# Attention and gated feed-forward in one kernel: two chunks' split weights kept across block borders, k and v laid out as four positions in 128 partitions plus a rest, three smaller stores

## The chip, the cores and the metric

One Trainium2 chip, one of its cores. The metric is device time in microseconds (us), the median of three runs of the program. The kernel before takes 946.88 us (945.2 to 952.26).

## What is computed

Inputs are q, k, v (8 batches x 8 heads x 576 positions x 64) and the weights of a gated feed-forward layer (512 to 1536 to 512), all f32.

```python
q_s = softmax(q, axis=-1)                  # over the 64 features
k_s = softmax(k, axis=2)                   # over the 576 positions
kv  = einsum('bhsd,bhse->bhde', k_s, v)
x   = einsum('bhsd,bhde->bhse', q_s, kv)   # -> 4608 tokens x 512
xn  = x / sqrt(mean(x*x) + 1e-06) * rms_g
out = (silu(xn @ w_gate) * (xn @ w_val)) @ w_out
```

A batch gives 576 tokens; the feed-forward layer (called the FFN here) works on nine blocks of 512 tokens.

## The kernel before, in words

**Precision.** Each f32 operand of a matmul is split in two halves, a high one (a cast to TensorE's fp32r type) and a low one (value minus high half), and each product is made of three matmuls: high by high, high by low, low by high. So the weights are split too, chunk by chunk.

**Order.** Nothing is scheduled by a compiler. A long string, ORDER, lists every step as `name.arguments`, with an engine behind a colon (S = SyncE, A = ScalarE, D = VectorE, P = GpSimd) where the step doesn't take its usual one. Each step issues its instructions when the string comes to it, so the string is the order of every engine and of each queue. Loads of q, k and v and most stores to memory go out on SyncE's queue (SP), one instruction after the other; one that has to wait holds up all behind it. In the program every DMA on SP also waits for the landing of the DMA eight places ahead of it on SP.

**FFN.** The first three blocks (0 to 2) are computed plainly: 36 steps s = 0 to 35, where block = s div 12 and the chunk of 128 of the 1536 hidden features is s mod 12. Step s has `f1.s` (gate and value products, L996), `g_mul`, `silu`, `h_mul`, `h_hi`, `h_lo` (the hidden values and their halves, L1008, L1005, L411, L1017) and `f2.s` (product with w_out, L1033). Before `f1.s`, the chunk's weights are split: `w_hi.s` (a cast of 128x1024, L411), `w_lo.s.0` and `w_lo.s.1` (two subtractions of 128x512, L920), and for `f2.s` `o_hi.s` (a cast of 128x512) and `o_lo.s` (a subtraction of 128x512, L928). The tiles `w` and `o` for them have two buffers each. In block 2 the chunks 6 to 11 (s = 30 to 35) don't split again: `w_back` and `o_back` read halves back that were kept in memory.

During block 1 (s = 12 to 23) the halves are also stored to memory: `w_keep.s` (L940, 1024 KB into `wd`, half of a slot for a pair of chunks) and `o_keep.s` (L944, 512 KB into `od`), together with sums of quarters of the weights (`s_add`, `s_hi`, `s_lo`, `s_keep`, L969 to L981) and copies of the raw weights (`r_keep`, L1254). The last six blocks run as three pairs with Strassen's scheme on these stored pieces, read back on GpSimd's queue. Of an odd chunk's two stored quarters, the first (A21) is read again only by `w_back`.

**Attention.** It runs in between, on batches 1 to 7 (batch 0 comes first, in another layout). For batch b and head pair g: `k_load` (three DMAs on SP, L505 and L509), `k_max` (DVE, L547), `k_tr` (a transposition on PE, L563), `k_top` (DVE maximum, tile `kx`, L568), `k_rows` (PE, L573), `k_sub` (DVE, L579), `k_exp` (ACT, L583), `k_mm` (PE, L600); `v_load` is four DMAs (L535, L536) and `v_ones` two memsets (L542, L543). The 576 positions of a head lie in 128 partitions as five positions each in 64 partitions and, in the other 64, four new positions and one taken twice, whose row in v's tile is zero. `q_load` is eight DMAs in runs of 128 bytes (L670), followed by `q_max` (DVE, L736), `q_exp` (ACT, L757), `q_mul` (POOL) and so on. `store` scales an output tile (ACT or DVE, L416) and stores it (SP, L1040).

Of the kernel before, what the change touches and what calls it, by code (L numbers as in the profile page):

```python
# [86 lines left out]
q_max2.2.2 n_rows.1 q_sub.2.2:P store.0.2:A k_top.2.1 g_mul.12 k_rows.2.1 s_lo.1.1:P k_mm.2.0 q_exp.2.2 k_sub.2.1
w_keep.13:S w_hi.14.0.2:A r_keep.1 f1.13.0 k_eps.2.0 q_half2.2.1 s_add.1.4:P k_load.2.2 k_exp.2.1 q_max.2.3 silu.12
k_rec.2.0 w_lo.14.0:P k_mm.2.1 v_ones.2.2 w_lo.14.1:D kv_hi.2.0:A q_half.2.3 s_add.2.1:P s_keep.1.1:S v_load.2.2
store.0.3:A h_mul.12 s_add.0.1:P g_mul.13 f1.13.1 h_hi.12:A q_sum.2.2 o_hi.13:A h_lo.12:P kv_lo.2.0 q_half2.2.2  # L90
s_add.0.3:P q_max2.2.3 q_sum2.2.2 q_sum2.2.1 k_eps.2.1 q_rec.2.2 k_rec.2.1 v_ones.2.3 o_lo.13:D q_sub.2.3:D k_load.2.3
s_lo.1.2:D q_rec.2.1 q_mul.2.1:P o_keep.13:S w_keep.14:S store.0.1:A s_hi.1.4:A silu.13 f2.12 kv_hi.2.1:A q_exp.2.3
f1.14.0 s_lo.1.4:D k_max.2.2 s_hi.2.1:A q_lo.2.0:P o_hi.15:A kv_lo.2.1 w_hi.15.0.2:A s_keep.1.2:S h_mul.13 k_tr.2.2
v_load.2.3 q_x.2.0 s_add.2.2:P k_top.2.2 q_sum.2.3 k_rows.2.2 x_sq.2.0 q_t.2.1 f1.14.1 o_lo.15:P x_hi.2.0:A k_sub.2.2
q_hi.2.1:A x_lo.2.0 q_mul.2.2:P k_exp.2.2 q_half2.2.3 h_hi.13:A q_lo.2.1:P g_mul.14 k_mm.2.2 silu.14 q_x.2.1
# [1382 lines left out]
```

## Time and profile before

| | us |
|---|---|
| median of 3 runs (lowest, highest) | 946.88 (945.2, 952.26) |
| profiled execution, its own time | 944.05 |
| its span, first to last instruction | 941.8 |
| PE (matmul) busy | 924.7 |
| DVE, ACT, POOL busy | 729.5, 467.4, 532.8 |
| mean granted TensorE clock | 0.997 |

The rows below come from the one profiled execution; times in them count from the start of its span. PE is TensorE, DVE VectorE, ACT ScalarE, POOL GpSimd. "SPq" is SP's queue of DMA issues. A row of the chain of work gives start, duration, and what ran.

### The profile page before, as it was taken

How to read it: one execution, taken by the hardware profiler on the slowest of the kernel's cores; microseconds unless marked ns; L12 is line 12 of the kernel's file. 1: busy time of each engine (PE TensorE's matmuls, PEld its weight loads, DVE VectorE, ACT ScalarE, POOL GpSimd, SP SyncE). 2: the span in 40 equal slices, each digit the busy share in tenths (PEclk: the TensorE clock that was granted, in tenths of full speed). 3: DMA queues.
4: the chain of work that ended last, by engine and by line, in shares of the span. 5: the costliest groups of instructions: out<-in, count | busy, mean ns of one | idle time of the engine just before them, and what ended most of it. 6: DMA issues, size and time to landing. Idle time of an engine off the chain costs nothing.

```text
span 941.8 us, 14336 instructions
## 1 busy us (share of the span) xinstructions
PE 924.7 (98%) x4621; PEld 748.9 (80%) x4621; DVE 729.5 (77%) x1526; ACT 467.4 (50%) x748; POOL 532.8 (57%) x546
## 2 busy tenths in 40 slices
PE   8999999999999998999999999999999999999998
PEld 6687877887877886888888888888888888888886
DVE  6989879988978996877877788775458975646586
ACT  4998848765678764655644364322215522111241
POOL 4887978877677995667764535433532423332403
PEclk9999999999999999999999999999999999999999
DMA  9997528989977999798995699888665778855255
GB/s 237 285 249 227 157 47 283 295 269 311 289 247 210 240 249 239 192 254 223 254 248 181 198 286 282 279 292 296 187 210 176 218 193 264 271 203 179 66 158 90
DMA packets 210298, 212.65 MB, mean 226 GB/s; under 512 B 132144, under 2 KB 171568, under 8 KB 205616
## 3 DMA queue, kind: packets, MB, share of 16 engines
q1 hardware_dynamic: 187568, 122.86, 47.7%
q0 software_dynamic: 16320, 88.09, 29.9%
q10 hardware_dynamic: 6336, 0.79, 0.6%
q8 instruction: 37, 0.61, 0.3%
q14 instruction: 37, 0.30, 0.1%
HBM read 161.35 MB, written 50.33 MB: 225 GB/s over the span
## 4 chain that ended last, share of the span: by engine, by line
PE 83%; DMA 7%; DVE 3%; ACT 2%; issue 2%; SPq 2%; POOL 0%; DVEq 0%; ACTq 0%
PE ps_gv L1145 18%; PE ps_gv L996 14%; PE ps_o L1145 12%; PE ps_o L1033 7%; PE ps_a L1145 7%; PE ps_o L1354 6%; PE ps_o L1238 4%; PE ps_a L1354 4%; PE ps_gv L1354 3%; DMA qt<-in_q_dram 2%; PE ps_a L1238 2%; PE ps_gv L1238 2%; DMA w<-in_v_dram 2%; PE ps_a L600 2%; PE ps_a L808 2%
## 5 line engine op out<-in xcount | busy, mean ns | idle before, releaser
L996 PE MATMUL ps_gv<-xh,w 128*128 128x512 f32 x576 | 191.8, 399 | 1.1 <-DVE gs L1008 1.1
L1145 PE MATMUL ps_gv<-x,ring 128*128 128x512 f32 x576 | 143.0, 392 | 0.0
L996 PEld LDWEIGHTS ps_gv<-xh,w 128*128 128x128 f32 x576 | 108.5, 188 | 26.9 <-DVE gs L1008 2.1
L1145 PEld LDWEIGHTS ps_gv<-x,ring 128*128 128x128 f32 x576 | 107.0, 188 | 23.0
L996 PE MATMUL ps_gv<-xl,w 128*128 128x512 f32 x288 | 112.6, 392 | 0.0
L1166 DVE TENSOR_TENSOR tmp<-tmp,ps_gv 128x512 f32<-128x512 f32 x84 | 57.3, 684 | 49.5 <-PE ps_gv L1145 47.8
L1145 PE MATMUL ps_o<-x,ring 128*128 128x512 f32 x360 | 85.1, 389 | 0.0
L1118 POOL DMA_DIRECT2D ring<-wd x54 | 31.0, 575 | 91.2 <-PE ps_o L1145 34.1
L1145 PEld LDWEIGHTS ps_o<-x,ring 128*128 128x128 f32 x360 | 67.6, 188 | 14.2
L1033 PE MATMUL ps_o<-o,hh 128*128 128x512 f32 x288 | 73.5, 396 | 0.0
L996 PEld LDWEIGHTS ps_gv<-xl,w 128*128 128x128 f32 x288 | 54.5, 189 | 10.7 <-issue 0.4
L1033 PEld LDWEIGHTS ps_o<-o,hh 128*128 128x128 f32 x288 | 52.9, 188 | 11.8 <-ACT ot L416 0.7
L1166 DVE TENSOR_TENSOR tmp<-tmp,ps_o 128x512 f32<-128x512 f32 x42 | 28.7, 685 | 29.1 <-PE ps_o L1145 25.7
L920 POOL TENSOR_TENSOR w<-w,w 128x512 fp32r<-128x512 f32 x34 | 45.9, 1359 | 8.2 <-ACT w L411 7.6
L411 ACT CAST hh<-gs 128x512 fp32r<-128x512 f32 x48 | 29.6, 617 | 30.4 <-DVE gs L1008 16.0
L1033 PE MATMUL ps_o<-o,hl 128*128 128x512 f32 x144 | 39.7, 399 | 4.3 <-DVE hl L1017 4.3
L1118 POOL DMA_DIRECT2D w<-wd x18 | 10.1, 559 | 58.0 <-PE ps_a L1145 37.8
L547 DVE TENSOR_REDUCE cm<-kt 128x128 f32<-128x640 f32 x28 | 36.7, 1312 | 3.1 <-DMA kt<-in_k_dram 3.0
L1145 PE MATMUL ps_a<-x,w 128*128 128x512 f32 x144 | 36.9, 392 | 0.0
L1017 POOL TENSOR_TENSOR hl<-gs,hh 128x512 fp32r<-128x512 f32 x21 | 28.1, 1339 | 15.2 <-DMA qt<-in_q_dram 6.0
L1145 PE MATMUL ps_a<-x,ring 128*128 128x512 f32 x144 | 36.7, 390 | 0.0
L1033 PEld LDWEIGHTS ps_o<-o,hl 128*128 128x128 f32 x144 | 27.4, 191 | 10.9 <-DVE hl L1017 4.7
(632 smaller groups left out, 2320.3 us busy)
## 6 DMA issues: line engine op xcount, KB each, us to landing
...
```

What stands on the lines that cost most here:

```text
L411: (e.copy if e is nc.scalar else e.tensor_copy)(dst, src)
L547: nc.vector.tensor_reduce(out=cm, in_=kt_[b, g].rearrange("p h j d -> p h d j"), axis=AX.X, op=ALU.max)
L600: nc.tensor.matmul(pk[h * D:(h + 1) * D, :D + 1], lhsT=ke[:, h, j], rhs=vt[:, j, h], start=(j == 0), stop=(j == CH - 1))
L920: on(nc.gpsimd).tensor_tensor(out=w[:, :, 1], in0=halves(s % NF, a, 1)[:, 0], in1=w[:, :, 0].bitcast(F32), op=ALU.subtract)
L996: nc.tensor.matmul(pd[s], lhsT=w[:, a, c // 2, m, c % 2 * P:c % 2 * P + P], rhs=X[j, c][x], start=(n == 1), stop=(n == 3 * NKT))
L1017: on(nc.gpsimd).tensor_tensor(out=hl, in0=g_[s], in1=h_[s][0].bitcast(F32), op=ALU.subtract)
L1033: nc.tensor.matmul(po[t], lhsT=a[:, t * P:(t + 1) * P], rhs=w, start=(i == 0 and n == 0), stop=(i == NF - 1 and n == len(terms) - 1))
L1118: nc.gpsimd.dma_start(t, src.rearrange("p a b f -> p (a b f)"))
L1145: nc.tensor.matmul(abc[p, i, m, b], lhsT=src[:, h, c * P:(c + 1) * P], rhs=operand(o, c, x), start=first and n == 0, stop=n == 5, skip_gro ...
L1166: nc.vector.tensor_tensor(out=dst, in0=ux[u + (src,)], in1=abc[u + (b,)], op=ALU.add)
L1238: nc.tensor.matmul(pa[p, t, k], lhsT=a[:, k * P:(k + 1) * P], rhs=w, start=(c == 0 and n == 0), stop=(c == NF - 1 and n == 2))
L1354: nc.tensor.matmul(qacc[p, b, x], lhsT=ws[l][x], rhs=h[m], start=first and i == 0 and n == 0, stop=i == NH - 1 and n == 2, skip_group_chec ...
```

## The change

1. A table CHUNK gives the chunk of each step. Block 1 runs chunks 10, 11, 2 to 9, 0, 1 instead of 0 to 11; blocks 0 and 2 are as before. So the last two chunks of a block are the first two of the next one, and `held(s)` makes steps 12 and 13 use the tiles of steps 10 and 11, and steps 24 and 25 those of 22 and 23. The 16 split steps (`w_hi`, two `w_lo`, `o_hi`, `o_lo`) of s = 12, 13, 24 and 25 are gone.
2. `k_load` is two DMAs instead of three: positions 0 to 511 as four per partition in all 128 partitions (both heads, runs of 1024 bytes), and the last 128 positions as a fifth one per partition (runs of 256 bytes; 64 of them are positions already loaded). Before, its runs were 1280 bytes. `v_load` is three DMAs instead of four, in the same layout: four positions in 128 partitions for each head, and the last 64 positions of both heads in the upper 64 partitions. The bytes are the same.
3. `w_keep` of an odd chunk that no `w_back` reads (chunks 1, 3 and 5) stores its second quarter alone: 512 KB instead of 1024 KB, three times.

The order of matmuls on PE is the same.

```diff
-silu.11 v_ones.2.0 v_load.2.0 q_load.2.3 w_hi.12.0.2:A o_hi.12:D o_hi.11:D n_sum.1 w_hi.13.0.2:A h_mul.11 w_lo.12.0:D
-o_lo.11:D kv_lo.1.2:P k_tr.2.0 w_lo.12.1:P f1.12.0 q_hi.2.0:A q_sub.2.1:P w_keep.12:S r_keep.5 kv_lo.1.3:P q_exp.2.1
+silu.11 v_ones.2.0 v_load.2.0 q_load.2.3 o_hi.11:D n_sum.1 h_mul.11 o_lo.11:D kv_lo.1.2:P k_tr.2.0 f1.12.0 q_hi.2.0:A
+q_sub.2.1:P w_keep.12:S r_keep.5 kv_lo.1.3:P q_exp.2.1 f1.12.1 r_keep.2 s_add.1.1:D r_keep.0 n_t.1 s_add.1.2:P
...
     def k_load(b, g):
...
-        head = k[b, hs].rearrange("h s d -> h (s d)")
-        low = head[:, :CH * LOW * D].rearrange("h (p e) -> p h e", p=LOW)
-        nc.sync.dma_start(kt[:LOW].rearrange("p h j d -> p h (j d)"), low)
-        for h in range(2):
-            first = k[b, 2 * g + h, CH * LOW - 1:CH * LOW]
-            over = bass.AP(tensor=first.tensor, offset=first.offset, ap=[[(CH - 1) * D, P - LOW], [1, CH * D]])
-            nc.sync.dma_start(kt[LOW:, h].rearrange("p j d -> p (j d)"), over)
+        nc.sync.dma_start(kt[:, :, :CH - 1].rearrange("p h j d -> p h (j d)"),
+                          k[b, hs, :REST].rearrange("h (p j) d -> p h (j d)", j=CH - 1))
+        nc.sync.dma_start(kt[:, :, CH - 1], k[b, hs, S - P:].rearrange("h p d -> p h d"))
...
-            nc.sync.dma_start(vt[:LOW, :, h, :D], src[:CH * LOW].rearrange("(p j) d -> p j d", j=CH))
-            nc.sync.dma_start(vt[LOW:, 1:, h, :D], src[CH * LOW:].rearrange("(p j) d -> p j d", j=CH - 1))
+            nc.sync.dma_start(vt[:, :CH - 1, h, :D], src[:REST].rearrange("(p j) d -> p j d", j=CH - 1))
+        nc.sync.dma_start(vt[P - S + REST:, CH - 1, :, :D], v[b, hs, REST:].rearrange("h p d -> p h d"))
...
+    CHUNK = [*range(NF), 10, 11, *range(2, 10), 0, 1, *range(NF)]
+    def held(s):
+        return s - 2 if s > 1 and CHUNK[s] == CHUNK[s - 2] else s
...
+    BACK = CHUNK[30:JP * NF]
     def w_keep(s):
-        i, odd = divmod(s % NF, 2)
+        i, odd = divmod(CHUNK[s], 2)
+        if odd and CHUNK[s] not in BACK:
+            on(nc.sync).dma_start(parts_of(i, A22, 1)[:, :, 0],
+                                  wh_[held(s)][:, :, 1].rearrange("p m b f -> p m (b f)").bitcast(F32))
+            return
         on(nc.sync).dma_start(parts_of(i, A21 if odd else A11, 2),
-                          wh_[s].rearrange("p m a b f -> p m a (b f)").bitcast(F32))
+                          wh_[held(s)].rearrange("p m a b f -> p m a (b f)").bitcast(F32))
...
     def f1(s, a, *part):
-        w = wh_[s]
+        w = wh_[held(s)]
```

Three places of the engines' orders follow; a row is the line, the operation, and its tiles (written, then read). Line numbers of after differ by a few.

On DVE, around the border of blocks 0 and 1 (the casts of `o` are `o_hi.12` and `o_hi.11`, L920 `w_lo`, L928 `o_lo.11`, L568 the maximum `kx` that `k_rows` waits for). Before:

```order
L411 CAST o<-w_91 128x512
L411 CAST o<-w_96 128x512
L1008 TENSOR_TENSOR gs<-ps_gv,gs 128x512
L920 TENSOR_TENSOR w<-w_91,w 128x2x256
L928 TENSOR_TENSOR o<-w_96,o 128x512
L969 TENSOR_TENSOR sums<-w_92 128x512
L920 TENSOR_TENSOR w<-w_91,w 128x2x256
L863 STREAM_TRANSPOSE sq<-ps_a 128x512
L568 TENSOR_REDUCE kx<-ps_a 128x1
```

After:

```order
L409 CAST o<-w_96 128x512
L1017 TENSOR_TENSOR gs<-ps_gv,gs 128x512
L930 TENSOR_TENSOR o<-w_96,o 128x512
L978 TENSOR_TENSOR sums<-w_92 128x512
L857 STREAM_TRANSPOSE sq<-ps_a 128x512
L562 TENSOR_REDUCE kx<-ps_a 128x1
```

Three instructions ahead of `kx` are gone, and nothing has come in their place.

On POOL, a little later in the same stretch (L1017 is `h_lo.11`, L928 `o_lo.12`, L920 `w_lo.13.0` and then `w_lo.14.0`, L753 `q_sub`, L969 and L978 the sums and their low halves). Before:

```order
L1017 TENSOR_TENSOR hl<-gs,hh 128x512
L928 TENSOR_TENSOR o<-w_91,o 128x512
L920 TENSOR_TENSOR w<-w_91,w 128x2x256
L753 TENSOR_TENSOR qt<-qt,sw 128x512
L978 TENSOR_TENSOR parts<-sums,parts 128x2x256
L969 TENSOR_TENSOR sums<-w_92,sums 128x512
L920 TENSOR_TENSOR w<-w_92,w 128x2x256
```

After:

```order
L1026 TENSOR_TENSOR hl<-gs,hh 128x512
L747 TENSOR_TENSOR qt<-qt,sw 128x512
L987 TENSOR_TENSOR parts<-sums,parts 128x2x256
L978 TENSOR_TENSOR sums<-w_92,sums 128x512
L922 TENSOR_TENSOR w<-w_92,w 128x2x256
```

`q_sub` now stands right behind `h_lo`; `w_lo.14.0` stays.

On SP's queue, from `w_keep.12` (L940; L1254 are `r_keep`, L944 `o_keep.12`, L1040 output stores, L505 and L509 a `k_load`, L535 and L536 a `v_load`, L981 `s_keep`). Before:

```order
L940 DMA wd_104<-w 128x2x1024
L1254 DMA rd_127<-w_96 256x1x512
L1254 DMA rd_124<-w_93 256x1x512
L1254 DMA rd_122<-w_91 256x1x512
L944 DMA od_110<-o 128x1024
L1040 DMA out_dram<-ot 128x512 x2
L940 DMA wd_104<-w 128x2x1024
L1254 DMA rd_123<-w_92 256x1x512
L505 DMA kt<-in_k_dram 64x2x320
L509 DMA kt<-in_k_dram 64x320 x2
L981 DMA wd_105<-parts 128x2x512
L535 DMA vt<-in_v_dram 64x5x64
```

After:

```order
L948 DMA wd_109<-w 128x2x1024
L1263 DMA rd_127<-w_96 256x1x512
L1263 DMA rd_124<-w_93 256x1x512
L1263 DMA rd_122<-w_91 256x1x512
L952 DMA od_120<-o 128x1024
L1049 DMA out_dram<-ot 128x512 x2
L948 DMA wd_109<-w 128x2x1024
L1263 DMA rd_123<-w_92 256x1x512
L501 DMA kt<-in_k_dram 128x2x256
L503 DMA kt<-in_k_dram 128x2x64
L990 DMA wd_105<-parts 128x2x512
L529 DMA vt<-in_v_dram 128x4x64 x2
```

The order of the stores is the same, into the slots of chunks 10 and 11 instead of 0 and 1; the load of k has one row fewer, and so has the load of v that follows.

## Rows read from the trace of the kernel before

**Rows 1.** The page, part 1: busy time, share and instructions of each engine.

```profile
PE 924.7 (98%) x4621; PEld 748.9 (80%) x4621; DVE 729.5 (77%) x1526; ACT 467.4 (50%) x748; POOL 532.8 (57%) x546
```

**Rows 2.** Busy time by window: start:end, length, engines' busy us, clock, DMA share, GB/s.

```profile
150.00:175.00 25.00, 23.15 (x154) 18.22 (x153) 23.83 (x67) 20.66 (x33) 21.55 (x23) 1.00 0.96 327
...
200.00:225.00 25.00, 22.68 (x105) 18.52 (x104) 18.77 (x37) 14.48 (x23) 14.59 (x16) 1.00 0.90 295
...
275.00:300.00 25.00, 24.72 (x132) 19.38 (x129) 22.56 (x53) 18.67 (x29) 18.06 (x20) 1.00 0.71 211
300.00:325.00 25.00, 24.61 (x148) 19.96 (x147) 21.96 (x67) 18.76 (x31) 23.28 (x26) 1.00 0.88 228
...
350.00:375.00 25.00, 20.73 (x101) 16.43 (x100) 16.84 (x40) 11.19 (x18) 13.76 (x16) 0.93 1.11 267
```

**Rows 3.** What PE waited for, whole span: us in total, times, longest.

```profile
PE ps_o L1033 <- DVE hl L1017: 4.3, 1, 4.3
PE ps_a L573 <- DVE kx L568: 3.6, 3, 2.3
...
PE ps_gv L996 <- DVE gs L1008: 1.1, 3, 0.7
```

**Rows 4.** Timeline of DVE around 150 us: start, duration, what.

```profile
142.33 0.76 DVE L411 CAST o<-w 128x512 fp32r<-128x512 f32 x2
...
143.88 0.92 DVE L920 TENSOR_TENSOR w<-w,w 128x512 fp32r<-128x512 f32 x1
...
147.05 0.68 DVE L920 TENSOR_TENSOR w<-w,w 128x512 fp32r<-128x512 f32 x1
...
152.83 0.25 DVE L568 TENSOR_REDUCE kx<-ps_a 128x1 f32<-128x128 f32 x1
```

**Rows 5.** The chain of work, 143 to 160 us: start, duration, what.

```profile
150.18 1.25 POOL o L928
151.43 0.91 POOL w L920
...
152.62 1.05 POOL qt L753
...
154.24 1.04 ACT w L411
```

**Rows 6.** The chain of work, 196 to 220 us.

```profile
207.18 0.46 SPq L670
...
209.60 1.27 SPq L509
...
210.92 2.75 DMA kt<-in_k_dram
...
218.36 0.32 PE ps_a L573
```

**Rows 7.** Timeline of SP's queue, 334 to 360 us: start, duration, what.

```profile
338.09 0.61 SPq L505 DMA_DIRECT2D kt<-in_k_dram  x1
...
340.35 17.83 SPq L670 DMA_DIRECT2D qt<-in_q_dram  x24
```

**Rows 8.** The chain of work, 326 to 374 us.

```profile
341.93 6.81 DMA qt<-in_q_dram
...
366.80 0.69 DVE st L736
```

**Rows 9.** DMA queues (packets, MB, share of 16 engines) and issues (KB, us to landing).

```profile
q1 hardware_dynamic: 187568, 122.86, 47.7%
...
kt<-in_k_dram SPq DMA_DIRECT2D x28, 160.0 KB, 5.5
kt<-in_k_dram SPq DMA_DIRECT2D x56, 80.0 KB, 4.9
```

**Rows 10.** The chain of work, 272 to 287 us.

```profile
276.50 3.25 DMA kt<-in_k_dram
...
285.10 2.12 PE ps_gv L996 x8
```

More of the change, by code (lines that the diff above doesn't have):

```diff
@@ L87 @@
[L87 to L95, printed above, removed]
+silu.11 v_ones.2.0 v_load.2.0 q_load.2.3 o_hi.11:D n_sum.1 h_mul.11 o_lo.11:D kv_lo.1.2:P k_tr.2.0 f1.12.0 q_hi.2.0:A
@@ new lines @@
+q_sub.2.1:P w_keep.12:S r_keep.5 kv_lo.1.3:P q_exp.2.1 f1.12.1 r_keep.2 s_add.1.1:D r_keep.0 n_t.1 s_add.1.2:P
+h_hi.11:A k_top.2.0 s_hi.1.1:A q_sum.2.1 h_lo.11:P k_rows.2.0 s_hi.1.2:A n_y0.1 f2.11 k_sub.2.0 n_y1.1 k_exp.2.0
+o_keep.12:S k_tr.2.1 store.0.0:A q_max2.2.2 n_rows.1 q_sub.2.2:P store.0.2:A k_top.2.1 g_mul.12 k_rows.2.1 s_lo.1.1:P
+k_mm.2.0 q_exp.2.2 k_sub.2.1 w_keep.13:S w_hi.14.0.2:A r_keep.1 f1.13.0 k_eps.2.0 q_half2.2.1 s_add.1.4:P k_load.2.2
+k_exp.2.1 q_max.2.3 silu.12 k_rec.2.0 w_lo.14.0:P k_mm.2.1 v_ones.2.2 w_lo.14.1:D kv_hi.2.0:A q_half.2.3 s_add.2.1:P
@@ new lines @@
+s_keep.1.1:S v_load.2.2 store.0.3:A h_mul.12 s_add.0.1:P g_mul.13 f1.13.1 h_hi.12:A q_sum.2.2 h_lo.12:P kv_lo.2.0
+q_half2.2.2 s_add.0.3:P q_max2.2.3 q_sum2.2.2 q_sum2.2.1 k_eps.2.1 q_rec.2.2 k_rec.2.1 v_ones.2.3 q_sub.2.3:D
+k_load.2.3 s_lo.1.2:D q_rec.2.1 q_mul.2.1:P o_keep.13:S w_keep.14:S store.0.1:A s_hi.1.4:A silu.13 f2.12 kv_hi.2.1:A
+q_exp.2.3 f1.14.0 s_lo.1.4:D k_max.2.2 s_hi.2.1:A q_lo.2.0:P o_hi.15:A kv_lo.2.1 w_hi.15.0.2:A s_keep.1.2:S h_mul.13
+k_tr.2.2 v_load.2.3 q_x.2.0 s_add.2.2:P k_top.2.2 q_sum.2.3 k_rows.2.2 x_sq.2.0 q_t.2.1 f1.14.1 o_lo.15:P x_hi.2.0:A
@@ L129 @@
-o_keep.23:S h_hi.23:A r_keep.4 o_hi.24:A s_lo.3.3:P q_load.4.2 k_rows.3.3 g_mul.24 k_tr.4.0 f1.24.1 k_top.4.0 silu.24
-k_sub.3.3 w_hi.25.0.2:A q_hi.3.3:D o_lo.24:D q_exp.4.0 w_lo.25.0:D k_rows.4.0 h_lo.23:D f2.23 s_lo.5.1:D s_hi.4.3:A
-q_sum.4.0 s_keep.5.1:S k_exp.3.3 s_lo.4.3:P q_max.4.1 s_keep.3.3:S w_hi.26.0.2:A q_half2.4.0 k_mm.3.3 w_lo.25.1:P
-store.1.2:A k_sub.4.0 f1.25.0 store.1.3:A q_sum2.4.0 k_eps.3.3 w_lo.26.0:P q_rec.4.0 k_exp.4.0 h_mul.24 k_load.4.1
-k_rec.3.3 h_hi.24:A q_mul.4.0:P kv_hi.3.3:A k_mm.4.0 o_hi.25:A q_lo.3.3:P q_t.4.0 f1.25.1 q_half.4.1 q_hi.4.0:A
@@ L134 @@
-q_load.4.3 o_lo.25:P store.1.0:A k_eps.4.0 kv_lo.3.3 store.1.1:A q_max.4.2 h_lo.24:P k_rec.4.0 q_max2.4.1 q_half.4.2
+w_lo.23.1:D f1.23.0 k_max.3.3 q_lo.3.2:P s_hi.4.1:A s_add.5.1:D s_hi.3.3:A q_sum.3.3 s_lo.4.1:P f1.23.1 w_keep.23:S
+q_half2.3.3 o_keep.22:S h_lo.22:P g_mul.23 q_load.4.1 n_cols.2 q_sum2.3.3 q_max.4.0 f2.22 x_cp.3.0:A q_half.4.0
+x_cp.3.1:A q_max2.4.0 q_rec.3.3 silu.23 k_max.4.0 q_mul.3.3:P q_x.3.2 o_hi.23:A s_keep.4.1:S k_tr.3.3 f1.24.0 x_sq.3.2
+k_top.3.3 o_lo.23:P h_mul.23 x_cp.3.2:A q_t.3.3 s_hi.5.1:A q_sub.4.0:P o_keep.23:S h_hi.23:A r_keep.4 s_lo.3.3:P
```

40 lines of the change are left out of this document (22 added, 18 removed).

## The prediction

> **What bounds the kernel now.** The first view is busy time by engine [rows 1]: PE is busy for 924.7 of 941.8 us, so at most 17 us of the span are not its own work, and the change leaves PE's work and its order as they are. What can be won is some of PE's idle time, and no more. The second view is busy time in stretches of 25 us [rows 2]. From 100 us on, PE is full in all stretches but five before the kernel's end. Its idle time there is 25.00 - 23.15 = 1.85 us (150 to 175), 25.00 - 22.68 = 2.32 (200 to 225), 0.28 (275 to 300), 0.39 (300 to 325) and 4.27 (350 to 375, where the granted clock falls to 0.93 too). The third view is what PE waited for [rows 3]: 4.3 us in one piece for `h_lo` (tile hl), 3.6 us in three for the keys' maximum (kx), the longest 2.3, and 1.1 us in three for hidden values (gs). All three name DVE, but each is a different story, and the rest of the work is to follow each wait back to what was late. After 375 us nothing that the change touches makes PE wait, and before 100 us the change hardly reaches.
>
> **The change, part by part.**
>
> *Split steps taken out.* Sixteen steps are gone; ACT loses casts of 128x1024 (1.04 us each [rows 5]), DVE and POOL subtractions of 128x512. DVE is busy 23.83 of 25 us and POOL 21.55 in the first bad stretch [rows 2], so here taking work away moves what is behind it.
>
> First wait, at 153 us. `k_rows` waits for the DVE maximum that begins at 152.83 [rows 4]. In the order of DVE this row stands behind `o_hi.12` (half of 0.76 us for two casts), `w_lo.12.0` (0.92) and `w_lo.13.1` (0.68), and DVE ran without a gap from there on. All three are removed: 0.38 + 0.92 + 0.68 = 1.98 us earlier. The wait itself is at most 3.6 - 2.3 = 1.3 us [rows 3], so it goes.
>
> Second wait, the one of 0.7 us for gs at about 158.6 us [rows 3]. Its chain [rows 5] runs over POOL's `o_lo.12` (1.25) and `w_lo.13.0` (0.91 on the chain) to `q_sub` at 152.62, and from there to ACT, where the cast of w at 154.24 and the work of the hidden values follow. Both POOL rows are removed, so the chain is 1.25 + 0.91 = 2.16 us earlier, more than the 0.7 waited. What is late next is the cast itself (`w_hi.14`): its buffer needs `w_keep.12` to have landed. That store used to wait for `w_lo.12` on DVE; now it stores a tile that has been ready since block 0, so it goes earlier, not later. I count all 1.85 us of this stretch.
>
> *Fewer DMAs for k and v.* At 218.36 PE waits its longest 2.3 us for kx. Followed back [rows 6], k's transfer lands late: its last part was issued at 209.60, took 2.75 us from 210.92, and SP had been issuing q's loads and stores one behind the other until then. So this is a queue that is late, not a transfer that is slow. The change takes one DMA from each `k_load` and one from each `v_load`. Between 152 us, where SP is last seen waiting for a producer, and this load there are five `k_load` and three `v_load` (the load itself counted): eight DMAs. One costs 0.61 us and 0.04 of issue between two [rows 6, 7], 0.65 in all, so this k is issued 8 x 0.65 = 5.2 us earlier. DVE's maximum then no longer waits for it, and the 2.32 us go. A bound from below: if SP were held elsewhere (a store whose tile comes late), the five removed on k alone still give 3.25 us, again more than 2.32.
>
> The same queue stays behind until about 292 us. PE's small wait at 285.10 [rows 10] comes from ACT, held by a store that SP put out late and by the k transfer of 3.25 us at 276.50. By then SP has nine of each load less, 18 x 0.65 = 11.7 us, and ACT also loses four casts of steps 24 and 25. I count the 0.28 and the 0.39 us of the two stretches, 0.67 in all.
>
> *The price of the new layout.* k's bytes are the same, but 256 runs of 1280 bytes become 256 of 1024 and 256 of 256. That is 28 x 256 = 7168 more packets. On this queue 187,568 packets take 47.7% of sixteen engines' span [rows 9], 0.477 x 16 x 941.8 / 187,568 = 0.038 us each, so 256 packets over 16 engines cost 0.6 us for each `k_load`. The bound below is nothing (the bytes are the same). The bound above is from q's loads, which come in runs of 128 bytes: 24 of them, three head pairs of 2 x 576 positions of two runs, are 6912 packets; they took from 340.35 until their last landing, 17.83 + 6.8 = 24.6 us [rows 7, 8], with the engines full [rows 2], 24.6 x 16 / 6912 = 0.057 us each, so 0.9 us for each `k_load`. Since most packets of this queue are short ones, I take the mean's 0.6. Where DMAs have room (shares of 0.7 to 0.96 in most stretches) it is hidden behind the earlier issue. Loads of 160 KB and 80 KB took 5.5 and 4.9 us to land [rows 9], hardly different for twice the bytes: their time is mostly not bytes. The Trainium skill ("DMA: Bandwidth & Descriptors", Specifications) asks for runs of at least 512 bytes for line rate, which speaks against the new fifth position; by that rule k's second transfer would be slow, and the gain on the queue smaller. The same page ("Rules for kernel authors") says that two transfers to disjoint partition halves serialize and one over 128 partitions should take their place, which speaks for it. No row of before has a k transfer in 256-byte runs, but v already comes in them.
>
> *The smaller stores.* Three times 512 KB less, on a queue whose landings matter only through the eight places. They lie in stretches that the terms above have counted already, so I give them nothing of their own; at most each takes one late landing off SP.
>
> *What stays.* The largest idle piece, 4.27 us in 350 to 375, is another matter. SP issues a `k_load` at 338.09, when PE frees its buffer, and behind it 24 q DMAs that take 17.83 us to issue [rows 7], each landing after some 6.8 us, with the DMA engines full (1.11 [rows 2]). `q_max` on DVE starts only at 366.80 [rows 8], and `h_lo` of step 33, in DVE's order behind it, comes late by 4.3. Here the change removes one DMA ahead of the q loads, 0.65 us, and adds 256 short packets, 0.6 us, to full engines. I take zero for it, with bounds of -0.65 and +0.9.
>
> **Sum.** 1.85 + 2.32 + 0.67 + 0 = 4.84 us. The profiled execution took 944.05 us, of which the span is 941.8, so it would take 939.2. It lies 2.83 under the median of the runs, 946.88; carried there, 946.88 - 4.84 = 942.04, rounded to 942.
>
> **The rivals.**
>
> *The last stall goes too.* If the queue's head start reaches the q loads (more than the one DMA, because landings come sooner with less behind them), the 4.27 us go as well, and the matmuls after the gap, which ran at a clock of 0.93, run full. 4.84 + 4.27 = 9.1, so 937.8; with the clock's part (0.07 of 20.7 us, 1.4) 936.4. Against it: the `k_load` at its head waits for PE, not for SP, so the head start is lost at 338 us. 13 in 100.
>
> *Nothing is won.* The waits removed are taken over by what was just behind them: DVE is still over 90% busy from 150 to 200 us, and q's loads wait on the same queue. Then it stays at 946 to 947. For it speaks that all three waits named the same engine; against it that each of the three chains loses two to five us where 0.7 to 2.3 are needed. A half of it is likelier than the whole: 944.5. For both, 24 in 100.
>
> *The short runs make it slower.* Place: the full stretch of 325 to 375 us, with three `k_load` just ahead of its q loads or among them, and 25 to 50 us, where two loads of batch 1 go out; each delay there is passed on to PE. In the first a us of gap costs more than itself, since the clock falls behind it: 1.4 us for 4.27, a third. So the price is (2 + 3 x 1.33) x 16 = 96 packets' time: 3.6 us at 0.038 us a packet, less than the 4.84 won, and 5.5 at 0.057, which makes the kernel 0.6 us slower: 947.5. It decides where a 256-byte packet costs more than 4.84 / 96 = 0.050 us. By the Trainium skill's rule on 512 bytes ("DMA: Bandwidth & Descriptors", Specifications) such a price is possible; the rows do not show it. 8 in 100.
>
> *The change doesn't do what it says* is excluded for the DMAs and the split steps, which the orders show as gone; that `w_keep.12` waits no longer is read from the program only.
>
> **How the numbers follow.** The forecast, 940 to 944, has 55 in 100; the last stall gone too 13; half or nothing won 24; slower through the short runs 8. The range leaves out the far end of each side: from 936 (the last stall and its clock) to 947.5 (the short runs at their upper bound). A measurement of this kernel can tell about 1% from no change, here 9.5 us. Faster by more than that (under 937.4) needs the last stall and the clock together: 9 in 100. Slower by more (over 956.3) needs nearly three times the price in that rival: 3 in 100. Within 1%: 88.
>
> **What the profile of the changed kernel would show.** PE full in 150 to 175 and 200 to 225 us; the wait for kx down from 3.6 us to under 0.5; SP's issues of the k load now at 208.75 some 5 us earlier against PE's work; the wait of 4.3 us for hl still there, near 362 to 368. Wrong would be: k's second DMA landing later than the old third one by more than 1 us, DVE's maximum over the keys waiting longer than now, or new waits on kx at 25 to 50 us. If the two early waits are still there though the rows ahead of them are gone, the chains were read wrongly.

## The result, and the profile after

The changed kernel takes 932.91 us (median of 6 runs, 932.23 to 933.66) against 946.33 for the kernel before (6 runs beside them, 945.02 to 952.26); the ratio is 0.9874, with a 95% interval of 0.9841 to 0.9907. That is 13.4 us, where 4.8 were forecast, and faster by a little over 1% where "within 1%" was. The profiled execution has a span of 930.7 us against 941.8. The difference of the two spans, 11.1 us, is less than that of the medians, since the profiled execution of before, 944.05 us, was one of its better ones: its 72 runs, those of the studies below included, lay anywhere from 937 to 954 us, and 22 of them were faster. (The ratios in this document leave out disturbed runs, 4 of these 72 and one of e3, and aren't the plain ratio of two medians; where the two differ, the traces carry the argument.)

The page of after, part 1, beside [rows 1]: PE has the same 4621 matmuls, but they took 4.2 us less (920.5 against 924.7), and its idle time is down from 17 us to 10. So not all of the 11.1 us are idle time.

```profile
PE 920.5 (99%) x4621; PEld 748.1 (80%) x4621; DVE 727.0 (78%) x1520; ACT 461.4 (50%) x741; POOL 522.4 (56%) x539
```

Busy time by window of after, columns as in [rows 2]:

```profile
150.00:175.00 25.00, 22.96 (x155) 18.48 (x154) 23.57 (x63) 20.76 (x33) 20.15 (x21) 1.00 0.96 319
200.00:225.00 25.00, 24.70 (x112) 20.08 (x111) 20.64 (x40) 16.24 (x25) 18.04 (x14) 1.00 0.96 311
275.00:300.00 25.00, 24.61 (x130) 20.02 (x129) 22.23 (x50) 19.54 (x32) 15.86 (x14) 1.00 0.65 195
300.00:325.00 25.00, 25.00 (x152) 20.64 (x151) 22.89 (x66) 19.01 (x29) 23.22 (x27) 1.00 0.89 237
350.00:375.00 25.00, 25.00 (x133) 20.61 (x132) 21.79 (x51) 18.68 (x32) 18.21 (x22) 1.00 0.87 251
```

Read against [rows 2], the stretch of 200 to 225 us is filled, as forecast. The stretch of 150 to 175 us, which I had counted as won, is no better (22.96 against 23.15). And the stretch of 350 to 375 us, which I had said would stay, is full, at full clock. What PE still waited for, whole span, beside [rows 3]:

```profile
PE ps_a L567 <- DVE kx L562: 1.4, 3, 0.7
PE ps_gv L1005 <- DVE gs L1017: 1.3, 1, 1.3
```

The wait of 4.3 us for hl is not in the list any more. In the stretch of 150 to 175 us, where both of the first two waits were to go, PE waits 0.74 us for kx and 1.29 for gs; before it was 0.94 and 0.72.

The matmuls are the same 4621 in the same order, so each can be compared with itself. The table gives how much earlier a matmul starts than in the trace of before, at five marks (time in before), and what was won between two marks; minus is later, or lost. A row is one trace of one kernel; the kernels e1 to e12 are described below.

| kernel | 91 us | 168 | 218 | 288 | 377 | won: start to 91 | 91-168 | 168-218 | 218-288 | 288-377 |
|---|---|---|---|---|---|---|---|---|---|---|
| forecast | | | | | | 0 | 1.85 | 2.32 | 0.67 | 0 |
| after | 1.26 | 1.60 | 3.76 | 4.90 | 11.03 | 1.26 | 0.34 | 2.16 | 1.14 | 6.13 |
| e1, layout alone | 1.28 | 1.35 | 3.34 | 4.48 | 10.62 | 1.28 | 0.07 | 1.99 | 1.14 | 6.14 |
| e8, layout, old count | 1.68 | 1.70 | 2.48 | 3.63 | 9.77 | 1.68 | 0.02 | 0.78 | 1.15 | 6.14 |
| e12, all but batch 1 | -1.11 | -1.13 | 0.87 | 2.03 | 8.18 | -1.11 | -0.02 | 2.00 | 1.16 | 6.15 |
| e6, after with one load in 5 | 0.67 | 0.90 | 3.05 | 4.21 | 1.50 | 0.67 | 0.23 | 2.15 | 1.16 | -2.71 |

The largest piece, 6.13 us, is the one that I had priced at nothing: 4.27 us of it are the wait, and 1.9 are matmuls just behind it: those of 512 columns took 0.80 and then 0.63 us in before (granted clock 0.66 in 370 to 375 us), the same ones 0.39 to 0.40 in after (1.00 in all stretches there). All the others together are 4.90 us, by chance the sum of the forecast, 4.84.

### The profile page after: what moved, and what is told of

Its sections match the earlier page's. It is cut to its first block, busy times and chain, and to the rows that moved or that the text cites. A ratio compares the mean times of both kernels' runs of the same rounds, so it can differ in the third digit from the quotient of the medians.

```text
span 930.7 us, 14213 instructions
## 1 busy us (share of the span) xinstructions
PE 920.5 (99%) x4621; PEld 748.1 (80%) x4621; DVE 727.0 (78%) x1520; ACT 461.4 (50%) x741; POOL 522.4 (56%) x539
## 3 DMA queue, kind: packets, MB, share of 16 engines
q1 hardware_dynamic: 193840, 121.29, 46.1%
## 4 chain that ended last, share of the span: by engine, by line
PE 95%; DVE 3%; DMA 1%; issue 0%; ACT 0%; POOL 0%; DVEq 0%; ACTq 0%; POOLq 0%
PE ps_gv L1005 20%; PE ps_gv L1154 18%; PE ps_o L1154 12%; PE ps_o L1042 10%; PE ps_a L1154 7%; PE ps_o L1363 6%; PE ps_o L1247 4%; PE ps_a L1363 4%; PE ps_gv L1363 3%; PE ps_a L594 2%; PE ps_a L802 2%; PE ps_a L1247 2%; PE ps_gv L1247 2%; PE ps_o L802 1%; PE ps_gv L476 1%; DMA wd<-w 1%
## 5 line engine op out<-in xcount | busy, mean ns | idle before, releaser
L1005 PEld LDWEIGHTS ps_gv<-xl,w 128*128 128x128 f32 x288 | 54.2, 188 | 10.6 <-issue 0.4
L922 POOL TENSOR_TENSOR w<-w,w 128x512 fp32r<-128x512 f32 x29 | 39.3, 1363 | 5.1 <-ACT w L409 5.0
L1154 PE MATMUL ps_gv<-x,w 128*128 128x512 f32 x144 | 35.1, 391 | 0.0
```

Source lines behind the costliest of these rows:

```text
L922: on(nc.gpsimd).tensor_tensor(out=w[:, :, 1], in0=halves(CHUNK[s], a, 1)[:, 0], in1=w[:, :, 0].bitcast(F32), op=ALU.subtract)
L1005: nc.tensor.matmul(pd[s], lhsT=w[:, a, c // 2, m, c % 2 * P:c % 2 * P + P], rhs=X[j, c][x], start=(n == 1), stop=(n == 3 * NKT))
L1154: nc.tensor.matmul(abc[p, i, m, b], lhsT=src[:, h, c * P:(c + 1) * P], rhs=operand(o, c, x), start=first and n == 0, stop=n == 5, skip_gro ...
```

## What the experiments were to tell apart

For the 6 us, three reasons stood against each other. Theory A, a crossing of two queues: the last of the 24 q loads on SP's queue is issued either before or after a read of 1024 KB that GpSimd's queue issues when PE frees its buffer; if after, it lands late, and all that stands behind it on DVE with it. Theory B, a long lead: less work since 150 us lets everything run ahead. Theory D, the form of k's transfers holds the DMA engines. The rows for A, in both traces: SP's last q issue, GpSimd's issue of the read, and DVE's `q_max` that needs the last q load (start, duration, what, idle before it).

Before:

```profile
357.74 0.43 SPq L670 DMA_DIRECT2D qt<-in_q_dram  x1
356.55 0.77 POOL L948 DMA_DIRECT2D w<-wd  x1 [2.40 <-PE ps_gv L996]
366.80 0.69 DVE L736 TENSOR_REDUCE st<-qt 128x16 f32<-128x512 f32 x1 [7.05 <-issue]
```

After:

```profile
351.20 0.43 SPq L664 DMA_DIRECT2D qt<-in_q_dram  x1
351.63 0.77 POOL L957 DMA_DIRECT2D w<-wd  x1 [2.40 <-PE ps_gv L1005]
353.95 0.67 DVE L730 TENSOR_REDUCE st<-qt 128x16 f32<-128x512 f32 x1
```

In before the last q load is issued 1.19 us after the read and lands so late that DVE sits idle 7.05 us; in after it is issued 0.43 us ahead of it, and DVE doesn't wait. The read itself hangs on PE and so moves with it. What moved is SP's side: PE stood 4.9 us earlier at that point, the last q issue 6.5.

## The parts of the change, one at a time

**e1: the layout alone.** `k_load`, `v_load` and `v_ones` of after in the kernel before; weights split and stored as before.

```diff
+        nc.sync.dma_start(kt[:, :, :CH - 1].rearrange("p h j d -> p h (j d)"),
+                          k[b, hs, :REST].rearrange("h (p j) d -> p h (j d)", j=CH - 1))
+        nc.sync.dma_start(kt[:, :, CH - 1], k[b, hs, S - P:].rearrange("h p d -> p h d"))
```

> The kernel before with the new layout of k and v alone (two DMAs for k, three for v); all weights are split and stored as before. Theory A (a crossing of two queues): the 4.3 us wait for hl hangs on whether the last q load of the 24 is issued before or after the 1024 KB read on GpSimd's queue that follows PE; before it was issued at 357.74, 1.2 us behind that read (356.55), after 0.4 us ahead of it (351.20 against 351.63). The k load ahead of the 24 takes 0.99 us instead of 2.26, so the layout alone turns the order round: the wait for hl is gone, and the wait of 2.3 us for kx as well; 9 to 11 us faster in the profile. Theory B (a long lead: SP and the engines ahead since 150 us through the split steps taken out): the layout alone gives the 2.3 us and part of the rest, 3 to 5 us, and a wait for hl of 2 us or more stays.

Measured: 933.08 us (932.72 to 933.97) against 948.04, ratio 0.9844 (0.9782 to 0.9907): the whole gain, and with it the small spread. There is no wait for hl in its trace, and the table above shows it within 0.5 us of after everywhere. The layout here is that of k and of v together; which of the two counts for how much was not tried apart. Of theory B's path (the split steps taken out) nothing is needed.

**e2: the reuse alone.** ORDER, CHUNK and `held` of after, with the old layout and full stores.

```diff
+    CHUNK = [*range(NF), 10, 11, *range(2, 10), 0, 1, *range(NF)]
+    def held(s):
+        return s - 2 if s > 1 and CHUNK[s] == CHUNK[s - 2] else s
```

> The kernel before with the reuse of two chunks' halves alone (block 1 in the order 10, 11, 2 to 9, 0, 1); old layout of k and v, stores of full size. Theory A: the wait of 4 us for hl stays, and that of 2.3 us for kx stays or shrinks by under 1; 0 to 1.5 us faster. Theory B: the wait for hl shrinks by more than half; 4 to 7 us faster.

Measured: 944.72 us (939.38 to 948.92), ratio 0.9966 (0.9930 to 1.0003): not told from before. What PE waited for in its trace:

```profile
PE ps_o L1042 <- DVE hl L1026: 3.5, 1, 3.5
PE ps_a L571 <- DVE kx L566: 3.4, 3, 2.2
PE ps_gv L1005 <- DVE gs L1017: 2.8, 2, 1.5
```

All three waits of [rows 3] are there, though 16 split steps are gone. Theory B falls.

**e3: the smaller stores alone.**

```diff
+        if odd and s % NF < 6:
+            on(nc.sync).dma_start(parts_of(i, A22, 1)[:, :, 0],
```

> The kernel before with the three smaller stores alone. Theory A: no change, within 0.5 us of before, the wait for hl of about 4 us there. Theory C (a transfer less on the DMA engines is what counts): up to 2 us faster and a shorter wait for kx at about 218 us.

Measured: 945.63 us (938.13 to 952.54), ratio 0.9978 (0.9937 to 1.0020): no change that can be told. But the execution that was profiled took 938.13, and its wait for hl was 0.3 us: with nothing changed near 350 us, this run had its last q issue 0.76 us behind the read (356.08 against 355.32). So a kernel with all loads in the old form sometimes escapes the gap by itself, which is the first sign of where the spread comes from.

**e4: two DMAs for k in the old layout.** The two upper transfers joined over both heads.

```diff
-        for h in range(2):
...
+        over = bass.AP(tensor=first.tensor, offset=first.offset, ap=[[(CH - 1) * D, P - LOW], [S * D, 2], [1, CH * D]])
+        nc.sync.dma_start(kt[LOW:].rearrange("p h j d -> p h (j d)"), over)
```

> The kernel before with k's two upper DMAs joined into one over both heads (64x2x320, runs of 1280 bytes, the old layout); v and all else as before. So k has two DMAs as in the change, without its runs of 256 bytes and in 64 partitions. Theory A by the count of DMAs (0.65 us each): the k load ahead of the 24 q loads takes 1.3 us instead of 2.26, the last q issue moves by about 0.65 to 1 us, less than the 1.2 it was behind, so a wait for hl of 2 to 4 us stays; the 2.3 us for kx go, as five DMAs less (3.25 us) are ahead of it: 2 to 4 us faster. If what counts is the form over 128 partitions (0.38 to 0.48 us an issue instead of 0.61): under 1.5 us faster and both waits there.

Measured: 945.10 us (940.95 to 951.15), ratio 0.9971 (0.9941 to 1.0002). Its profiled run, 951.15, had the last q issue 1.84 us behind the read and the longest wait for hl of all, 6.5 us. 28 DMAs fewer on SP don't bring the gain. Its trace has 0.74 us between 168 and 218 us, about a third of what after has there; that of e3 has 0.75.

**e8: the new layout with the old count.** Three DMAs for k, four for v, in the new layout.

```diff
-        nc.sync.dma_start(kt[:, :, :CH - 1].rearrange("p h j d -> p h (j d)"),
-                          k[b, hs, :REST].rearrange("h (p j) d -> p h (j d)", j=CH - 1))
+        for h in range(2):
+            nc.sync.dma_start(kt[:, h, :CH - 1].rearrange("p j d -> p (j d)"),
+                              k[b, 2 * g + h, :REST].rearrange("(p j) d -> p (j d)", j=CH - 1))
...
+            nc.sync.dma_start(vt[P - S + REST:, CH - 1, h, :D], src[REST:])
```

> The kernel before with the new layout, but with as many DMAs as before: three for k (one per head in 128 partitions, and the rest), four for v. If the form is what counts (128 partitions; 0.38 to 0.48 us an issue instead of 0.61): 933 to 936, small spread, the k load ahead of the 24 q loads takes 1.3 to 1.5 us. If the count is what counts (0.65 us each, 56 more): 942 to 948, with the waits for kx (2 us) and hl (over 3 us) back. By theory A alone the last q issue would be 0.6 to 1 us behind the read, at the edge: a wait for hl of 0 to 3 us.

Measured: 934.54 us (934.15 to 936.80), ratio 0.9876 (0.9805 to 0.9946). With as many DMAs as before, the new form is 10.7 us below the 945.19 of the kernel before beside it, and 1.5 above e1. So the form gives most of the gain; the count gives the rest, and the table says where: 0.78 us instead of 1.99 between 168 and 218 us, where a wait for kx of 1.5 us stays.

## The crossing, moved on purpose

**e6: the changed kernel with one load in pieces.** The `k_load` ahead of the 24 q loads, and no other, is five DMAs instead of two.

```diff
+        if (b, g) == (5, 2):
+            for h in range(2):
+                for p in (slice(0, 64), slice(64, 128)):
+                    nc.sync.dma_start(kt[p, h, :CH - 1].rearrange("p j d -> p (j d)"),
+                                      k[b, 2 * g + h, :REST].rearrange("(p j) d -> p (j d)", j=CH - 1)[p])
```

> The changed kernel with one load cut up: k_load.5.2, just ahead of the 24 q loads, is 5 DMAs instead of 2 (halves of the partitions, per head, same bytes and runs). SP is some 1.3 to 1.9 us later there and nowhere else. Theory A: the last q issue falls 0.9 to 1.5 us behind the 1024 KB read instead of 0.4 ahead, and a wait for hl of 2 to 5 us comes back: 936 to 939, with more spread than the 1.5 us of after. Theory D: a delay of at most 1.9 us that is hidden: 933 to 934, no wait for hl.

Measured: 942.30 us (939.02 to 946.40, 10 runs): 9.4 us more than after, whose slowest run is 933.66. The same three kinds of rows of its trace:

```profile
354.80 0.61 SPq L670 DMA_DIRECT2D qt<-in_q_dram  x1
352.31 0.77 POOL L963 DMA_DIRECT2D w<-wd  x1 [2.39 <-PE ps_gv L1011]
364.00 0.69 DVE L736 TENSOR_REDUCE st<-qt 128x16 f32<-128x512 f32 x1 [8.35 <-DMA qt<-in_q_dram]
```

And what PE waited for there (us in total, times, longest):

```profile
PE ps_o L1048 <- DVE hl L1032: 5.7, 1, 5.7
```

The q loads began 2.4 us later against PE than in after, the last was issued 2.49 us behind the read, DVE stood 8.35 us and PE 5.7. In the table nothing else differs from after by more than 0.6 us; between 288 and 377 us 8.8 us are lost. Three DMAs more in one load cost nine microseconds.

**e5: the kernel before with q ahead.** One word of ORDER: `k_load.5.2` stands behind the first 8 of the 24 q loads, so SP doesn't sit idle until PE frees k's buffer.

```diff
-x_nm.3.3:D k_mm.5.0 q_sum.5.1 w_back.33 b_hi.0.3.1:A n_lo.4:P k_rows.5.1 silu.31 q_half2.5.1 k_load.5.2 f2.30
+x_nm.3.3:D k_mm.5.0 q_sum.5.1 w_back.33 b_hi.0.3.1:A n_lo.4:P k_rows.5.1 silu.31 q_half2.5.1 f2.30
...
-q_load.5.3 f1.32.0 o_back.32 q_sum2.5.2 b_lo.0.0.0:D h_hi.31:A q_t.5.1 h_lo.31:P q_rec.5.2 q_hi.5.1:A n_t.4 q_lo.5.1:P
+q_load.5.3 k_load.5.2 f1.32.0 o_back.32 q_sum2.5.2 b_lo.0.0.0:D h_hi.31:A q_t.5.1 h_lo.31:P q_rec.5.2 q_hi.5.1:A n_t.4 q_lo.5.1:P
```

> The kernel before with one word moved in ORDER: k_load.5.2 stands behind the first 8 of the 24 q loads instead of ahead of them, so that the queue issues q while PE still holds k's buffer. Nothing of the change is in it. Theory A (the crossing of the last q load with the 1024 KB read on GpSimd's queue): so far the last q issue against that read gave: 0.4 us ahead (after), 0.5 and 0.8 us behind (e1, e3): no or 0.3 us of wait for hl; 1.1, 1.2, 1.8 us behind (e2, before, e4): 3.5, 4.3, 6.5 us. Here the last q issue comes some 4 us ahead of the read: no wait for hl, 4 to 7 us faster than before (about 941 to 943). The spread of the runs, some 15 us in before, stays in its early part. Theory D (the gap belongs to the old form of k's transfers, which hold the DMA engines): the wait stays at 3 us or more and the time at 946 to 948.

Measured: 941.36 us (938.07 to 947.10) against 945.19 beside it, ratio 0.9978 (0.9936 to 1.0020), so by the times alone not told from before. In its trace the last q load is issued at 357.86 and the read at 358.11, and there is no wait for hl: between 288 and 377 us its PE gains 6.1 us, as much as after. Theory D, for which the wait had to stay, falls with this: all k loads have the old form here, as in e3. (e6 alone couldn't rule it out, as its pieces, too, are transfers over 64 partitions.) The last q issue is only 0.25 us ahead of the read, not some 4 as expected: the 24 q loads with the k load between them took until 357.86.

The gain doesn't all last. Near 455 us DVE waits again for a q load, and PE behind it, so that 2.85 of the 6.1 us are lost there (a row of DVE's timeline, and the longest of the waits of PE: us in total, times, longest):

```profile
453.80 0.69 DVE L736 TENSOR_REDUCE st<-qt 128x16 f32<-128x512 f32 x1 [3.36 <-DMA qt<-in_q_dram]
PE ps_gv L1145 <- DVE tmp L1166: 1.4, 1, 1.4
```

Neither before nor after has a wait of PE there.

**e9: one load of 28 in the new layout**, the same `k_load.5.2` and its v. A function picks the pairs in the new layout:

```diff
+    def flat(b, g):
+        return (b, g) == (5, 2)
```

> The kernel before with one head pair of 28 in the new layout: batch 5, pair 2, whose k load stands just ahead of the 24 q loads. Theory A (the crossing): that load issues in 1.0 us instead of 2.3, so the last q issue moves from 1.2 us behind the 1024 KB read to about 0.1 ahead of it: the wait for hl is gone or under 0.5 us, about 5 to 6 us faster than before by the median (940 to 942), the waits for kx stay, and the runs still spread by some 8 us, from the early part. Theory F (all loads add up): a gain of a 28th, 0.5 us.

Measured: 939.81 us (936.93 to 950.71) against 945.59, ratio 0.9980 (0.9938 to 1.0023). In its trace that load issues in 0.39 and 0.48 us, the last q issue is 0.77 us behind the read, and there is no wait for hl; 5.0 us are won between 288 and 377 us. It isn't safe, though: six runs lie at 936.9 to 940.7 and four at 945.2 to 950.7, and the four have a mean granted clock of 0.994 to 0.996, the six of 0.997 to 1.000. In the traces a lower clock goes with the gap on PE (0.93 in the stretch of the gap in [rows 2], 1.00 there in after), so I take the four to be runs in which the crossing was lost; that is not shown, as none of the four was profiled, and another wait, such as that of e5 near 455 us, is not excluded.

All 14 traces together, in order of the last q issue against the read:

| trace | last q issue after the read, us | its issue to landing, us | wait for hl, us |
|---|---|---|---|
| after | -0.43 | 1.9 | 0 |
| e5 | -0.25 | 2.1 | 0 |
| e8 | -0.13 | 1.9 | 0 |
| e12 | 0.30 | 1.6 | 0 |
| e7 | 0.34 | 1.7 | 0 |
| e1 | 0.46 | 4.0 | 0 |
| e11 | 0.58 | 4.4 | 0 |
| e3 | 0.76 | 5.3 | 0.3 |
| e9 | 0.77 | 5.1 | 0 |
| e10 | 0.94 | 8.1 | 3.3 |
| e2 | 1.09 | 8.1 | 3.5 |
| before | 1.19 | 8.8 | 4.3 |
| e4 | 1.84 | 10.6 | 6.5 |
| e6 | 2.49 | 9.1 | 5.7 |

Up to 0.8 us it costs 0.3 us at most, from 0.9 on three microseconds and more, whatever part of the change the kernel has. The landing of that load goes up in steps, from about 2 us to 4 or 5 to 8 and more; what lies between was not seen. PE has enough other work to cover the first step, not the second. How long all 24 of q's transfers took to land (min, median, max), in before:

```profile
DMA to landing us min/median/max: 2.5/5.0/8.8
```

and in after:

```profile
DMA to landing us min/median/max: 1.9/5.3/6.9
```

The median is no shorter in after; it is the longest that differs. In before the longest, 8.8 us, is the last one: issued at 357.74, it is what DVE waited for until 366.8. Behind the read of 1024 KB GpSimd's queue has two of 768 and two of 512 KB, all issued within 5 us. The first two of the five land 5.7 and 9.4 us behind the first issue, the last q load 10.0, the other three 12.0 to 16.2: it lands among them, behind two. The trace's records of single packets show how: in the 1 us that begins 6 us behind the read's issue, GpSimd's queue moved 48 packets with 384 KB and SP's 49 with 6 KB, all of 128 bytes. The Trainium skill ("DMA: Bandwidth & Descriptors", Queues, rings and completion order) says that a DMA engine takes turns between its queues packet by packet; with short packets in one queue and long ones in the other that gives the short ones few bytes a turn. These counts agree with it, one record of the one queue to one of the other. No run changed q's packets or the reads themselves, so what makes the landing go up in steps stays open.

## The early part

**e10: batch 1 alone in the new layout**, 4 pairs of 28.

```diff
+    def flat(b, g):
+        return b == 1
```

> The kernel before with batch 1 alone (4 of 28 pairs) in the new layout; its loads go out between 12 and 70 us, when the DMA engines are full. If the old form in this part costs time and spread (PE was 0.9 us later at 72 us in before than after, and 2.7 to 4.0 later still in the profiles of e2 and e4): 2 to 4 us faster by the median (942 to 945), PE at its 72 us mark as in after (71.0), the wait for hl still there and with it a spread of some 6 us. If the early part varies for another reason: no change, 945 to 947.

Measured: 940.90 us (935.62 to 948.75), ratio 0.9960 (0.9925 to 0.9995). PE is 1.75 us earlier than in before at 91 us, the wait for hl is there (3.3 us).

**e11: batch 1 and the pair of e9.**

```diff
+    def flat(b, g):
+        return b == 1 or (b, g) == (5, 2)
```

> Both of the last two: batch 1 and the pair of batch 5 in the new layout, 5 of 28. If these two places carry the change: 935.5 to 937.5 with a spread of under 3 us; what is missing to 933 is the 2 us of the wait for kx at 218 us and some 0.7 us near 285. If the gain needs all loads: 941 to 945.

Measured: 937.88 us (936.26 to 945.54), ratio 0.9945 (0.9912 to 0.9978). By the medians five loads of 28 give 7.7 us, by the ratio 5; the whole change gave 13.4. In its trace 6.0 us come between 288 and 377 us and 1.27 before 91, but 3.05 are lost again near 455 us, as in e5 and again at a q load (DVE sits idle 2.95 us for it): the loads there are still in the old form. In e1, e6, e7 and e8, with the whole layout, at most 0.1 us are lost after 377 us, in after nothing. One run of seven may still have lost the crossing, by its clock (945.54, 0.993).

**e12: all but batch 1.**

```diff
+    def flat(b, g):
+        return b > 1
```

> The kernel before with all pairs but those of batch 1 in the new layout. Theory A with the early part: no wait for hl, the kx wait at 218 us gone, but the early part as in before: 935 to 938 with a spread of 4 us or more. If the early part doesn't hang on batch 1's form: 933 to 934.5, spread under 2 us, as with the whole layout.

Measured: 935.57 us (933.79 to 936.80), ratio 0.9913 (0.9882 to 0.9944). The table shows it equal to e1 in every part but the first, where it is 2.4 us later at 91 us. So in these two traces batch 1's form is worth 2.4 us at the start. The other traces agree: in all seven with the new form in batch 1 PE is 0.7 to 1.8 us ahead of before at 91 us, and in the seven with the old form 0 to 4.0 behind. (Of the 1.7 us of e8 0.9 and of the 1.8 of e10 0.4 stem from the first 10 us, before any load of batch 1 is issued.) SP's timeline there, the first k load of batch 1 and the first four q loads behind it. Before:

```profile
12.89 0.73 SPq L505 DMA_DIRECT2D kt<-in_k_dram  x1
13.66 1.90 SPq L509 DMA_DIRECT2D kt<-in_k_dram  x2
18.33 5.01 SPq L684 DMA_DIRECT2D qt<-in_q_dram  x4
```

After:

```profile
11.91 0.69 SPq L501 DMA_DIRECT2D kt<-in_k_dram  x1
12.64 0.78 SPq L503 DMA_DIRECT2D kt<-in_k_dram  x1
18.34 1.74 SPq L678 DMA_DIRECT2D qt<-in_q_dram  x4
```

After, four q loads that took 5.01 us to issue take 1.74. But that doesn't go with the form: from the first to the end of the fourth it is 3.5 us in e1 and 3.3 in e12, and in after SP was a microsecond ahead already at its first k load. The difference between e12 and e1 is made at 72 us, where PE waits in e12 and not in e1 (the wait of PE as above, then start, duration, what):

```profile
PE ps_gv L1013 <- DVE gs L1025: 1.7, 1, 1.7
61.14 8.39 DMA w<-in_moe_w_gate_dram
```

The second row is of the chain that ends with this wait: a load of w_gate on SP's queue. In the seven traces with the new form it is issued at 58.6 to 60.1 us and landed at 64.6 to 67.7; in the seven with the old one it is issued at 60.7 to 64.1 and landed at 68.4 to 72.4. PE's wait there is 0.1 us at most in the first, and 1.4 to 2.4 in five of the second (0.15 in before, none in e3). So with the old form in batch 1 SP's queue is behind at this place, and weights come late; by which of its loads it falls behind was not followed up. In the traces of e2 and e4 another 1 to 2 us are lost before 20 us; why is open. None of this was in the forecast.

## The stretch that didn't move

**e7: the changed kernel with `w_lo.14.1` later.** On DVE it stands behind `h_mul.12` and `g_mul.13`.

```diff
-k_exp.2.1 q_max.2.3 silu.12 k_rec.2.0 w_lo.14.0:P k_mm.2.1 v_ones.2.2 w_lo.14.1:D kv_hi.2.0:A q_half.2.3 s_add.2.1:P
-s_keep.1.1:S v_load.2.2 store.0.3:A h_mul.12 s_add.0.1:P g_mul.13 f1.13.1 h_hi.12:A q_sum.2.2 h_lo.12:P kv_lo.2.0
+k_exp.2.1 q_max.2.3 silu.12 k_rec.2.0 w_lo.14.0:P k_mm.2.1 v_ones.2.2 kv_hi.2.0:A q_half.2.3 s_add.2.1:P
+s_keep.1.1:S v_load.2.2 store.0.3:A h_mul.12 s_add.0.1:P g_mul.13 w_lo.14.1:D f1.13.1 h_hi.12:A q_sum.2.2 h_lo.12:P kv_lo.2.0
```

> The changed kernel with one word moved: w_lo.14.1 on DVE (1.76 us there) stands behind h_mul.12 and g_mul.13 instead of ahead of them. In the changed kernel PE waits 1.3 us for h_mul.12 at 157.6, and DVE ran through without idling from PE's transposition at 147.9, w_lo.14.1 in it. If that chain on DVE is what holds PE: the 1.3 us shrink to 0.5 or less and the time falls by 0.5 to 1.3 us, to about 932. If it is ACT (silu.12 ends at 156.0) or f1.14 then waits for w_lo.14.1: no change, 933.

The rows behind it, DVE's timeline in after (start, duration, what, idle before it):

```profile
148.01 0.82 DVE L573 TENSOR_TENSOR kt<-kt,ps_a 128x640 f32<-128x640 f32 x1 [2.28 <-PE ps_a L567]
...
151.29 0.25 DVE L562 TENSOR_REDUCE kx<-ps_a 128x1 f32<-128x128 f32 x1
...
154.38 1.76 DVE L922 TENSOR_TENSOR w<-w,w 128x512 fp32r<-128x512 f32 x1
...
156.89 0.69 DVE L1017 TENSOR_TENSOR gs<-ps_gv,gs 128x512 f32<-128x512 f32 x1
```

DVE has the time that the removed split steps gave it, and spends 2.28 us of it waiting for `k_rows` on PE (L567). From 148.01 on it runs without a pause, 13 instructions long to kx, and PE waits again. Behind that, `w_lo.14.1` took 1.76 us where the same subtraction took 0.80 in before, and `h_mul.12` stood behind it.

Measured for e7: 932.54 us (932.33 to 933.50, 4 runs), against 932.91 for after: not told apart. In the trace the wait for gs falls from 1.3 to 0.5 us and PE is 0.83 us earlier at 158 us, 0.3 at the end. So the chain on DVE is what holds PE there, and the longer subtraction was part of it.

## Why the prediction was wrong, step by step

- **"After 375 us nothing that the change touches makes PE wait".** Right: what is won at 377 us (11.03) is won at the end (11.04).
- **"What can be won is some of PE's idle time, and no more".** Wrong: of the 11.1 us between the two spans 6.9 are idle time, and 4.2 are the same matmuls taking less, 1.9 of them behind the gap.
- **First and second wait, 1.85 us.** Wrong; 0.34 measured, and the two waits together are 2.03 us in after, 1.66 in before. The failed step is "DVE ran without a gap from there on. All three are removed: 1.98 us earlier". It took the distance on DVE for a gain and didn't ask what a DVE instruction further on waits for: `k_rows` on PE, whose place among PE's matmuls had not moved. Three instructions fewer became 2.28 us of idle DVE. The chain over POOL failed in the same way: POOL sits idle 4.31 us ahead of `q_sub` in after. The profile names a result of PE there, but `q_sub` reads DVE's `sw`, which ends at 150.71 us, and starts at 150.79: it stands behind the same chain on DVE. The prediction's own sign for this, early waits that are still there though the rows ahead of them are gone, came.
- **The wait for kx at 218 us, 2.32 us.** Right in place and size (2.16). The reason was half right: that the queue is late, yes. But the price of 0.65 us a DMA was not what it turned on: with the old count the new form still gives 0.78 us (e8), and with the old form and 28 DMAs fewer it is 0.74 (e4).
- **Near 285 us, 0.67 us.** 1.14 measured up to 288 us, the same with the ACT casts still there (e1), and 1.13 and 1.14 in e3 and e4, so neither the casts nor the new layout are needed for it. The wait of 0.39 us in 300 to 325 us, counted as won, is still there, at 296.75 us.
- **The price of the layout, 0.6 us for each k load.** Wrong: about nothing. Per packet I had 0.038 us from the mean of the queue. With the layout alone (e1, the bytes as before) the queue carries 193,840 packets instead of 187,568 and they take no more time in all, 0.472 x 931.2 = 440 us of sixteen engines against 0.477 x 941.8 = 449. By the trace's packet records the mean packet of 1280 bytes took 0.078 us on SP's queue in before, and in e1 one of 1024 took 0.054 and one of 256 took 0.020, the two together 0.074. With it falls the slower rival, which needed more than 0.050 for a packet of 256 bytes. The 512-byte rule of the Trainium skill ("DMA: Bandwidth & Descriptors", Specifications) speaks of a cost of short transfers: per byte the packet of 256 is the dearer one in e1, 0.079 ns against 0.053, but it costs the new layout nothing against packets of 1280 bytes. The page's other rule ("Rules for kernel authors"), one transfer over 128 partitions instead of two over halves, is the one that the runs bear out (e8: 934.54 us with as many DMAs as before); that halves serialize, the page's reason, no run here shows.

The queue in e1:

```profile
q1 hardware_dynamic: 193840, 122.86, 47.2%
```

- **"What stays": 4.27 us, priced at 0 with bounds of -0.65 and +0.9.** This is the miss, and the step that failed: 6.13 us, the 4.27 and some 1.9 of slower matmuls behind the gap. The shift was mis-sized, and the way from shift to price was wrong. I took 0.65 us off for one DMA; the k load ahead of q went from 2.26 us (338.09 to 340.35, [rows 7]) to 0.99, as its DMAs also issue faster (duration in ns min/median/max, two lines of before):

```profile
L505 SPq DMA_DIRECT2D kt<-in_k_dram x28: 606/624/1373, 12.9 to 491.3; - x28
...
L509 SPq DMA_DIRECT2D kt<-in_k_dram x56: 473/603/1483, 13.7 to 493.2; - x56
```

and of after:

```profile
L501 SPq DMA_DIRECT2D kt<-in_k_dram x28: 368/407/1355, 11.9 to 479.7; - x28
...
L503 SPq DMA_DIRECT2D kt<-in_k_dram x28: 385/478/1317, 12.6 to 480.4; - x28
```

And I let the price be as large as the shift. It isn't: the last q load either lands ahead of the other queue's reads or among them, and a shift of 1.6 us against PE (1.27 from the k load, the rest from the q loads' own issue) decides over 6. I had seen that the engines were full there, and hadn't asked with whose bytes.
- **The rivals.** "The last stall goes too" was the one that came (936.4 against 932.91), but not by the way given. My argument against it, that a head start is lost where k waits for PE, is right for the lead of the queue (the k load there is issued 4.9 us earlier, as PE is), and overlooked that the k load itself got shorter. "Nothing is won" describes the first stretch alone.
- **The start.** That the change "hardly reaches" the time before 100 us was wrong: 1.26 us in the two traces, 2.4 between e12 and e1.
